# Weight tiles through GpSimd's queue, and a new order of work in the first two pairs of a fused attention and MLP kernel

## Chip, cores and metric

The kernel runs on one core of one Trainium2 chip. The metric is device time in microseconds (us) of one execution. The kernel before took 503.27 us, the median of three runs (502.56 to 503.57). The profile shown here is of one more execution.

## What is computed

Attention, then two feed-forward blocks on its output, all in float32 at the interface:

```
q, k, v: 2 x 12 heads x 448 x 64;  scale = 1/8
scores = scale * q @ k.T, causal mask (-1e9), softmax, @ v      # per head
x  = heads joined: 896 tokens x 768
h  = max(max(x @ w1, x @ w2), x @ w3);   y = h @ w_out          # 768 x 768 each
r  = max(y @ w_in, 0);  g = s * r * r + b                        # 768 x 2048
out = g @ w_out2                                                 # 2048 x 768
```

## The kernel before

**Tiles.** Two heads make a pair (12 pairs); a pair's q and k lie as one tile `R`, 128 partitions (2 heads x 64) by 2 x 448. Each float32 operand of a product is split into a rounded high part and a low remainder, and a product is the sum of three: high x high, low x high, high x low (`PARTS`). For a pair the tile `HL` holds -scale*q high, its low, k high and its low. `split_now` makes it for pair 0, in two column ranges (0 to 256, 256 to 448), `split_hi_early`/`split_lo_early` for pair 1, `scaled`, `split_hi` and `split_lo` for later pairs: GpSimd scales q in place (`R<-R`), VectorE casts the high parts (`CAST HL<-R`, L309), GpSimd subtracts the low parts (L92) and copies the tail columns into a block-diagonal tile `bd` (L296).

**Scores.** Query rows go in three tiles of 128 (tile 0, 1, 2) and a tail of 64 rows of both heads together. Tiles 0 and 1 lie in the PSUM bank pair `B`, tile 2 in `A`, the tail in `C`; each has one buffer, so the next pair's mask product (L350, L358, L365), which opens a bank, waits until ScalarE has read the old one. Per pair: masks and score products on TensorE, row minima of the negated scores on VectorE (`mx`, L396), exponentials with row sums on ScalarE (`p`, L408), 16 transposes on TensorE (L435) in four groups of four, copies of these (`PT`, three by ScalarE, one by VectorE, L441), products with V into the bank `o` (L451, L455, L460).

**The division.** Row sums are inverted, transposed into PSUM (L480), copied to `rows` (L487), sent by DMA to a DRAM row `rcd` (L488, L489), and from there by DMA to all partitions as `rb` (L497); VectorE multiplies `o` by `rb` into `xf` (L506), which frees `o` for the next product with V, and GpSimd splits `xf` into the `x` that the feed-forward part reads.

**Order.** Everything is written out by hand; each engine runs its instructions in that order. `step(s)` does, for s = 0 to 13, the scores of pair s (`new`), transposes of pair s-1 (`old`), products with V of pair s-2 (`out`), and the multiplication by `rb` of pair s-3; splitting of pair s+2 (`nxt`) and the scaling of pair s+3 lie beside them. All loads are issued by SyncE (SP) in program order: the pairs' `R` (L268), V in 42 pieces (L289, `V_LOADS` says how many at which place of a step), the weights' raw tiles `wraw` (`fetch_w`, L129, 768 KB each). SP has eight semaphores for its DMAs in turn, so an issue also waits for the DMA eight issues earlier. Within the attention part six raw tiles are fetched: at step 0 and at steps 1, 4, 8, 10, 11 (`FETCH`). In steps 1 to 13 four weight tiles are decoded between the attention work (`MID`, `END`).

**Feed-forward part.** From 93 us to the end TensorE runs the products of L698 and L807; the other 50 raw tiles are fetched by SP as decoding proceeds. `keep_busy` issues products on constants: `WARM` = 10 at the start, `BUSY` = 7 in step 0.

Of the kernel before, what the change touches and what calls it, by code (L numbers as in the profile page):

```python
# [14 lines left out]
ALU = mybir.AluOpType  # L15
# [8 lines left out]
TQ = 128  # L24
NQ = 3
# [14 lines left out]
V_LOADS = ((7, 7), (2, 5), (3, 4), (3, 0), (3, 0), (3, 0), (3, 0), (2, 0))  # L40
FILL = {12: (3, 5), 13: (0, 4)}
WARM = 10
BUSY = (7,)
# [7 lines left out]
def kernel(  # L51
# [73 lines left out]
    def fetch_w():  # L125
        if w_src:
            src = w_src.pop(0)
            raw = wr_p.tile([128, DM], I64, tag="wraw", name="wraw")
            nc.sync.dma_start(out=raw, in_=src)  # L129
            raws.append(raw)  # L130
# [101 lines left out]
    def attention():  # L232
        with ExitStack() as c2:
# [88 lines left out]
            def split_lo_early(p):  # L322
                HL, R = pair[p]["HL"], pair[p]["R"]
                nc.vector.scalar_tensor_tensor(
                    out=HL[:, 1], in0=R[:, 0], scalar=-scale, in1=HL[:, 0].bitcast(F32),
                    op0=ALU.mult, op1=ALU.subtract,
                )
                sub_lo(nc.vector, HL[:, 3], R[:, 1], HL[:, 2])

            def split_now(p, a, b, eng):  # L330
                HL, R = pair[p]["HL"], pair[p]["R"]
                q, k = (R[:, n, a:b] for n in range(2))
                qh, ql, kh, kl = (HL[:, n, a:b] for n in range(4))
                nc.vector.tensor_scalar(out=qh, in0=q, scalar1=-scale, scalar2=None, op0=ALU.mult)
                nc.scalar.copy(out=kh, in_=k)
                nc.vector.scalar_tensor_tensor(
                    out=ql, in0=q, scalar=-scale, in1=qh.bitcast(F32),
                    op0=ALU.mult, op1=ALU.subtract,
                )
                sub_lo(eng, kl, k, kh)  # L340
# [34 lines left out]
            def scores_ab(p, i):  # L375
                HL = pair[p]["HL"]
                n = (i + 1) * TQ
                for a, c in PARTS:
                    for h in range(2):
                        nc.tensor.matmul(  # L380
                            at(p, i)[:, h], HL[hs[h], a, i * TQ:n], HL[hs[h], 2 + c, 0:n],
                            start=False, stop=(a, c) == PARTS[-1], skip_group_check=True,
                        )
# [133 lines left out]
            for p in range(1, 4):  # L517
                load(p)
# [17 lines left out]
            split_now(0, 0, CUT, nc.vector)  # L536
            split_now(0, CUT, S, nc.gpsimd)
            both_tails(0)
            split_hi_early(1)
            first = early_products()  # L540
# [10 lines left out]
            def step(s):  # L551
# [4 lines left out]
                if new is not None:  # L556
                    results(new)
                    if new == 0:
                        mask_b(new)
                        scores_ab(new, 0)  # L560
                        scores_ab(new, 1)
                        mask_a(new)
                        scores_ab(new, 2)
                    else:
                        mask_a(new)
                        if new > 2:
                            mask_b(new)
                        scores_ab(new, 2)
                    if new == 2:
                        mask_b(new)  # L570
                    if new > 1:
                        scores_ab(new, 1)
                        scores_ab(new, 0)
                    if new != 1:
                        mask_c(new)
                        scores_c(new)
                else:
                    early(FILL[s][0])
                if old is not None:
                    transposes(old, 0)  # L580
                    transposes(old, 1)
                if new == 1:
                    mask_b(new)
                    scores_ab(new, 1)
                    scores_ab(new, 0)
                    mask_c(new)
                    scores_c(new)
                if new == 0:
                    for i in (0, 1, 2, NQ):
                        minima(new, i)  # L590
                    split_lo_early(1)
                    both_tails(1)
                    for n in (2, 3):
                        scaled(n)
                    for V in vs[:2]:
                        nc.gpsimd.memset(V[D:128, :, :, NQ, :], 0.0)
                elif new is not None:
                    minima(new, 2)
                if old is not None:
                    inverses(old)  # L600
                if new == 1:
# [3 lines left out]
                    for V in vs[2:]:  # L605
# [5 lines left out]
                if new == 1:  # L611
                    pt_copy(old, 0, nc.scalar)
                    pt_copy(old, 1, nc.scalar)
                    exps(new, 2)
# [22 lines left out]
                if new is not None:  # L637
                    for i in (1, 0) if new == 1 else (0, 1):
                        exps(new, i)
                if new == 0:  # L640
                    exps(new, 2)
# [6 lines left out]
                if new == 0:  # L648
                    load_v(loads[0])
# [5 lines left out]
                else:  # L655
                    fetch_w()
                load_v(loads[1])
                if s in FETCH:
                    fetch_w()
# [3 lines left out]
                if new == 1:  # L663
# [3 lines left out]
                    scaled(s + 3)  # L667
                if old is not None:
# [211 lines left out]
```

## Time and profile before

| what | value |
|---|---|
| median of the runs | 503.27 us |
| the profiled execution | 502.06 us |
| its span | 500.3 us |
| TensorE busy | 493.3 us (99%) |
| VectorE / ScalarE / GpSimd busy | 340.5 / 282.9 / 71.4 us |
| granted TensorE clock over the span | 0.999 |
| DMA moved, mean | 58.34 MB, 117 GB/s |

The span runs from the first to the last instruction; 1.76 us of the execution lie outside it. Engines work at the same time, so busy times don't add up. GpSimd's 71.4 us all lie in the first 97 us. In rows of a timeline the bracket at the end is idle time of that engine just before the row, and what ended it. A step of the attention part is told by TensorE's first mask product of it: step 1 starts at 10.03 us, step 2 at 14.89, steps 3 to 9 at 21.88, 28.26, 35.86, 43.10, 49.50, 55.87 and 62.29.

### The profile page before, as it was taken

What the parts mean: (1) busy time and instruction counts of PE and PEld (TensorE: products, weight loads), DVE (VectorE), ACT (ScalarE), POOL (GpSimd) and SP (SyncE); (2) the same over time, 40 slices, a digit from 0 to 9 for tenths busy, and PEclk for the clock granted to TensorE, in tenths of its full rate; (3) what the DMA queues carried; (4) which work ended last, traced back from release to release, by engine and by line L of the source; (5) the groups of instructions that cost most, each with busy time, mean ns of one, the idle gap of its engine ahead of it and who ended that gap; (6) DMA issues with size and microseconds to landing.
All of it is one profiled execution on the core that took longest, in us unless ns stands there. A gap on an engine that the chain in (4) does not pass through costs nothing.

```text
span 500.3 us, 7557 instructions
## 1 busy us (share of the span) xinstructions
PE 493.3 (99%) x2909; PEld 452.7 (90%) x2909; DVE 340.5 (68%) x512; ACT 282.9 (57%) x527; POOL 71.4 (14%) x103
## 2 busy tenths in 40 slices
PE   8999999999999999999999999999999999999997
PEld 4877888899999999999999999999999999999996
DVE  5778896665857667587677888888888644484401
ACT  5988977444445254444546878888786432253101
POOL 6988992300000000000000000000000000000000
PEclk9999999999999999999999999999999999999999
DMA  5777534223324231333223323332333323261003
GB/s 170 225 215 226 151 102 117 103 91 127 126 75 148 94 126 64 126 128 126 101 89 126 127 73 118 126 104 85 127 126 109 119 89 128 88 220 56 1 0 111
DMA packets 26212, 58.34 MB, mean 117 GB/s; under 512 B 13548, under 2 KB 17600, under 8 KB 26176
## 3 DMA queue, kind: packets, MB, share of 16 engines
q1 hardware_dynamic: 26032, 57.76, 35.2%
q8 instruction: 23, 0.38, 0.3%
q14 instruction: 13, 0.11, 0.1%
q10 hardware_dynamic: 144, 0.10, 0.1%
HBM read 55.05 MB, written 2.80 MB: 116 GB/s over the span
## 4 chain that ended last, share of the span: by engine, by line
PE 91%; DMA 2%; DVE 2%; SPq 2%; ACT 1%; POOL 1%; issue 0%; DVEq 0%; ACTq 0%
PE m L698 58%; PE m L807 23%; PE t L435 3%; PE o L451 2%; ACT p L408 1%; PE o L455 1%; SPq L289 1%; PE A L380 1%; PE C L388 1%; PE B L380 1%; DMA rcd<-rows 1%; DMA rb<-rcd 1%; DMA R<-in_qk_dram 1%; POOL HL L92 0%; PE o L460 0%
## 5 line engine op out<-in xcount | busy, mean ns | idle before, releaser
L698 PE MATMUL m<-x,whi 128*128 128x448 f32 x816 | 232.0, 366 | 0.0
L698 PEld LDWEIGHTS m<-x,whi 128*128 128x128 f32 x816 | 153.1, 188 | 12.3 <-ACT p L408 0.2
L698 PE MATMUL m<-x,wlo 128*128 128x448 f32 x408 | 149.0, 365 | 0.0
L807 PE MATMUL m<-whi,g 128*128 128x384 f32 x448 | 114.0, 334 | 0.0
L184 ACT CAST whi<-wa 128x768 fp32r<-128x768 f32 x56 | 46.7, 833 | 67.0 <-PE m L807 43.8
L698 PEld LDWEIGHTS m<-x,wlo 128*128 128x128 f32 x408 | 76.6, 188 | 6.0
L807 PEld LDWEIGHTS m<-whi,g 128*128 128x128 f32 x448 | 81.0, 188 | 0.0
L144 ACT ACTIVATE wa<-wraw 128x768 f32<-128x768 f32 x56 | 50.6, 904 | 52.3 <-DVE wlo L92 52.3
L92 DVE TENSOR_TENSOR wlo<-wa,whi 128x768 fp32r<-128x768 f32 x56 | 53.3, 953 | 38.4 <-ACT whi L184 38.4
L807 PE MATMUL m<-wlo,g 128*128 128x384 f32 x224 | 74.8, 334 | 0.0
L179 DVE CUSTOM_DVE_ANT_0 wa<-wa,wr 128x1536 uint16<-128x1536 uint16 x56 | 53.6, 957 | 1.9
L172 DVE SCALAR_TENSOR_TENSOR wa<-wraw,wa 128x768 int32<-128x768 int32 x56 | 53.7, 959 | 0.0
L147 ACT ACTIVATE wr<-wraw 128x768 int32<-128x768 uint32 x56 | 50.6, 904 | 0.0
L807 PEld LDWEIGHTS m<-wlo,g 128*128 128x128 f32 x224 | 42.0, 188 | 0.0
L705 DVE TENSOR_TENSOR t<-t,m 128x448 f32<-128x448 f32 x24 | 14.9, 621 | 38.7 <-PE m L698 38.7
L698 PE MATMUL m<-h,whi 128*128 128x448 f32 x144 | 40.9, 365 | 0.0
L166 DVE TENSOR_SCALAR wa<-wa 128x768 int32<-128x768 int32 x56 | 32.2, 575 | 1.8
L92 POOL TENSOR_TENSOR HL<-R,HL 128x448 fp32r<-128x448 f32 (+1 forms) x21 | 29.9, 1443 | 3.2 <-DVE HL L309 2.1
L792 ACT ACTIVATE r<-m 128x448 f32<-128x448 f32 x32 | 17.4, 544 | 22.2 <-PE m L698 22.2
L698 PEld LDWEIGHTS m<-h,whi 128*128 128x128 f32 x144 | 27.1, 188 | 2.1
L158 DVE TENSOR_SCALAR wa<-wa 128x768 f32<-128x768 f32 x52 | 28.7, 552 | 0.0
L781 DVE SCALAR_TENSOR_TENSOR r<-m,r 128x448 f32<-128x448 f32 x32 | 20.0, 625 | 12.3 <-ACT r L792 12.3
(85 smaller groups left out, 551.2 us busy)
## 6 DMA issues: line engine op xcount, KB each, us to landing
wraw<-in_w_dram SPq DMA_DIRECT2D x56, 768.0 KB
R<-in_qk_dram SPq DMA_DIRECT2D x11, 448.0 KB
rb<-rcd SPq DMA_DIRECT2D x24, 112.0 KB
out_dram<-o SPq DMA_DIRECT2D x13, 192.0 KB
v<-in_v_dram SPq DMA_DIRECT2D x4, 96.0 KB
v<-in_v_dram SPq DMA_DIRECT2D x2, 168.0 KB
v<-in_v_dram SPq DMA_DIRECT2D x6, 48.0 KB
v<-in_v_dram SPq DMA_DIRECT2D x2, 144.0 KB
```

The source lines that it names most:

```text
L92: eng.tensor_tensor(out=lo, in0=full, in1=hi.bitcast(F32), op=ALU.subtract)
L144: nc.scalar.activation(out=e["f"], in_=e["high"].bitcast(F32), func=ACTF.Abs)
L147: nc.scalar.activation(out=e["r"], in_=e["low"].bitcast(U32), func=ACTF.Copy, scale=2.0 ** -29)
L158: nc.vector.tensor_scalar(out=e["f"], in0=e["f"], scalar1=UNDER, scalar2=OVER, op0=ALU.max, op1=ALU.min)
L166: nc.vector.tensor_scalar(out=a, in0=a, scalar1=3, scalar2=0x3FFFFFF8, op0=ALU.logical_shift_left, op1=ALU.bitwise_and,)
L172: nc.vector.scalar_tensor_tensor(out=e["a"], in0=e["high"], scalar=-0x40000000, in1=e["a"], op0=ALU.bitwise_and, op1=ALU.bitwise_or,)
L179: nc.vector.tensor_tensor(out=e["a"], in0=e["a"], in1=e["r"], op=ALU.add)
L184: nc.scalar.copy(out=e["hi"], in_=e["f"])
L698: nc.tensor.matmul(p, wt[w][:, ws], cols(act[i], a, b), start=(i == 0 and n == 0), stop=(i == len(act) - 1 and n == 2),)
L781: nc.vector.scalar_tensor_tensor(out=r, in0=p, scalar=0.0, in1=r, op0=ALU.max, op1=ALU.mult)
L792: after(0, lambda: nc.scalar.activation(out=r, in_=p, func=ACTF.Relu))
L807: nc.tensor.matmul(acc[t][:, 0:EH], gt[f][:, a, ts], w[:, ws], start=(f == 0 and n == 0), stop=(f == KG - 1 and n == 2),)
```

## The change

Raw weight tiles that were fetched within the attention part (six of 56) are issued by GpSimd, in its own queue of DMAs, and no longer by SP. V's pieces are loaded in another distribution: three of pair 0's pieces between the loads of pairs 1 and 2, four between those of pairs 2 and 3, and ten at step 0 after pair 4's load; none behind `rb` in step 2. The second column range of pair 0 has its scaled q made by ScalarE and its low k by VectorE (before: VectorE, GpSimd). Pair 0's score products for tiles 0 and 1 run the two parts that need the high k for both tiles, and then the third part. Minima and exponentials of pair 0 go tile by tile in the order 0, 2, 1, and the tail's minimum stands between the two subtractions for pair 1. In step 1 the scores of `B` stand ahead of pair 0's first eight transposes, and the exponentials of `A` ahead of ScalarE's two copies. The zeroing of V's unused rows moves to steps 1 to 3. `BUSY` is 5.

```diff
-V_LOADS = ((7, 7), (2, 5), (3, 4), (3, 0), (3, 0), (3, 0), (3, 0), (2, 0))
+V_LOADS = ((0, 10), (3, 5), (3, 0), (3, 0), (3, 0), (3, 0), (3, 0), (2, 0))
-BUSY = (7,)
+BUSY = (5,)
-    def fetch_w():
+    def fetch_w(queue=nc.sync):
-            nc.sync.dma_start(out=raw, in_=src)
+            queue.dma_start(out=raw, in_=src)
...
                     op0=ALU.mult, op1=ALU.subtract,
                 )
+                minima(0, NQ)
                 sub_lo(nc.vector, HL[:, 3], R[:, 1], HL[:, 2])
...
-            def split_now(p, a, b, eng):
+            def split_now(p, a, b):
-                nc.vector.tensor_scalar(out=qh, in0=q, scalar1=-scale, scalar2=None, op0=ALU.mult)
                 nc.scalar.copy(out=kh, in_=k)
+                if a:
+                    nc.scalar.mul(out=qh, in_=q, mul=-scale)
+                    sub_lo(nc.vector, kl, k, kh)
+                else:
+                    nc.vector.tensor_scalar(
+                        out=qh, in0=q, scalar1=-scale, scalar2=None, op0=ALU.mult
+                    )
...
-                sub_lo(eng, kl, k, kh)
+                if not a:
+                    sub_lo(nc.vector, kl, k, kh)
...
-            def scores_ab(p, i):
+            def scores_ab(p, *tiles):
+                for parts in (PARTS[:2], PARTS[2:]):
+                    for i in tiles:
+                        n = (i + 1) * TQ
+                        for a, c in parts:
...
-            for p in range(1, 4):
-                load(p)
+            load(1)
+            load_v(3)
+            load(2)
+            load_v(4)
+            load(3)
...
-            split_now(0, 0, CUT, nc.vector)
-            split_now(0, CUT, S, nc.gpsimd)
+            split_now(0, 0, CUT)
+            split_now(0, CUT, S)
             both_tails(0)
             split_hi_early(1)
+            fetch_w(nc.gpsimd)
...
-                        scores_ab(new, 0)
-                        scores_ab(new, 1)
+                        scores_ab(new, 0, 1)
...
+                if new == 1:
+                    mask_b(new)
+                    scores_ab(new, 1)
+                    scores_ab(new, 0)
                 if old is not None:
                     transposes(old, 0)
                     transposes(old, 1)
                 if new == 1:
-                    mask_b(new)
-                    scores_ab(new, 1)
-                    scores_ab(new, 0)
                     mask_c(new)
                     scores_c(new)
                 if new == 0:
-                    for i in (0, 1, 2, NQ):
+                    for i in (0, 2, 1):
                         minima(new, i)
+                        exps(new, i)
...
                 if new == 1:
+                    exps(new, 2)
                     pt_copy(old, 0, nc.scalar)
                     pt_copy(old, 1, nc.scalar)
-                    exps(new, 2)
...
-                else:
-                    fetch_w()
                 load_v(loads[1])
-                if s in FETCH:
-                    fetch_w()
...
+                if s in FETCH:
+                    fetch_w(nc.gpsimd)
+                if 2 <= s < len(vs):
+                    nc.gpsimd.memset(vs[s][D:128, :, :, NQ, :], 0.0)
```

TensorE's queue at the start of step 1 (`A`, `B`, `C` are pair 1's banks, `t` pair 0's transposes), before:

```order
L350 LDWEIGHTS identb
L350 MATMUL A<-tri,identb 128x128
L380 MATMUL A<-HL 128x384 x6
L435 MATMUL t<-ident,p_133 128x128 x8
L358 LDWEIGHTS identb
L358 MATMUL B<-tri,identb 128x256
L358 LDWEIGHTS identb
L358 MATMUL B<-tri,identb 128x256
L380 MATMUL B<-HL 128x256 x6
L380 MATMUL B<-HL 128x128 x6
L365 LDWEIGHTS identb
L365 MATMUL C<-tri_106,identb 128x64
```

and now:

```order
L358 LDWEIGHTS identb
L358 MATMUL A<-tri,identb 128x128
L390 MATMUL A<-HL 128x384 x6
L366 LDWEIGHTS identb
L366 MATMUL B<-tri,identb 128x256
L366 LDWEIGHTS identb
L366 MATMUL B<-tri,identb 128x256
L390 MATMUL B<-HL 128x256 x6
L390 MATMUL B<-HL 128x128 x6
L445 MATMUL t<-ident,p_133 128x128 x8
L373 LDWEIGHTS identb
L373 MATMUL C<-tri_106,identb 128x64
```

The eight transposes, which need all exponentials of pair 0's tiles and the tail, stand behind `B`'s scores.

GpSimd's queue from pair 1's high parts to the scaling of pair 4 (`v_112` to `v_115` are the four groups of V), before:

```order
L296 TENSOR_SCALAR HL<-R 128x448 x2
L296 TENSOR_SCALAR bd_108<-HL 64x2x64 x2
L296 TENSOR_SCALAR R<-R 128x448 x2
L596 MEMSET v_112 64x2x64
L596 MEMSET v_113 64x2x64
L92 TENSOR_TENSOR HL<-R,HL 128x448 x2
L296 TENSOR_SCALAR bd_109<-HL 64x2x64 x2
L606 MEMSET v_114 64x8x64
L606 MEMSET v_115 64x12x64
L92 TENSOR_TENSOR HL<-R,HL 128x448 x2
L296 TENSOR_SCALAR bd_107<-HL 64x2x64 x2
L296 TENSOR_SCALAR R<-R 128x448
```

and now:

```order
L296 TENSOR_SCALAR HL<-R 128x448 x2
L129 DMA wraw<-in_w_dram 128x768
L296 TENSOR_SCALAR bd_108<-HL 64x2x64 x2
L296 TENSOR_SCALAR R<-R 128x448 x2
L92 TENSOR_TENSOR HL<-R,HL 128x448 x2
L296 TENSOR_SCALAR bd_109<-HL 64x2x64 x2
L619 MEMSET v_112 64x2x64
L619 MEMSET v_113 64x2x64
L92 TENSOR_TENSOR HL<-R,HL 128x448 x2
L296 TENSOR_SCALAR bd_107<-HL 64x2x64 x2
L296 TENSOR_SCALAR R<-R 128x448
L129 DMA wraw<-in_w_dram 128x768
```

Two DMA issues have come in, and the zeroing of groups 114 and 115 has gone to later steps. Four more issues follow, at the ends of steps 4, 8, 10 and 11.

SP's queue around the first two divisions, before:

```order
L289 DMA v_114<-in_v_dram 32x4x64
L129 DMA wraw<-in_w_dram 128x768
L488 DMA rcd<-rows 7x128
L489 DMA rcd<-rows 1x64
L268 DMA R<-in_qk_dram 128x896
L289 DMA v_114<-in_v_dram 32x4x64
L289 DMA v_114<-in_v_dram 80x4x64 x2
L497 DMA rb<-rcd 64x448 x2
L289 DMA v_114<-in_v_dram 48x4x64 x2
L289 DMA v_114<-in_v_dram 64x4x64 x2
L488 DMA rcd<-rows 7x128
```

and now:

```order
L289 DMA v_114<-in_v_dram 80x4x64 x2
L289 DMA v_114<-in_v_dram 48x4x64
L498 DMA rcd<-rows 7x128
L499 DMA rcd<-rows 1x64
L268 DMA R<-in_qk_dram 128x896
L289 DMA v_114<-in_v_dram 48x4x64
L289 DMA v_114<-in_v_dram 64x4x64 x2
L507 DMA rb<-rcd 64x448 x2
L498 DMA rcd<-rows 7x128
```

The first `rcd` in each is pair 1's, the last pair 2's. The raw tile ahead of pair 1's `rcd` and the four pieces of V between pair 1's `rb` and pair 2's `rcd` are gone from there.

## Rows read from the trace of the kernel before

**Rows 1.** Waits of TensorE, 0 to 130 us: total us, times, longest.

```profile
PE o L451 <- DVE xf L506: 1.9, 2, 1.1
...
PE A L350 <- ACT p L408: 0.6, 1, 0.6
```

**Rows 2.** Stretches: length; busy PE, PEld, DVE, ACT, POOL; clock; DMA share, GB/s.

```profile
6.00:8.00 2.00, 2.00 (x14) 1.22 (x13) 1.99 (x5) 0.86 (x5) 0.58 (x2) 1.00 0.92 321
...
15.00:22.00 7.00, 6.87 (x69) 5.37 (x67) 4.79 (x11) 6.97 (x26) 5.86 (x11) 1.00 0.70 199
...
28.30:35.90 7.60, 6.52 (x68) 5.36 (x66) 5.60 (x11) 6.22 (x20) 5.73 (x8) 1.00 0.58 147
35.90:43.10 7.20, 6.42 (x67) 5.29 (x65) 5.67 (x11) 6.17 (x20) 5.83 (x8) 1.00 0.91 222
...
49.50:55.90 6.40, 6.40 (x68) 5.34 (x66) 5.41 (x11) 6.15 (x20) 6.16 (x8) 1.00 0.65 172
```

**Rows 3.** Timeline of DVE around the divisions and casts: start, length, instruction, idle before.

```profile
27.58 0.28 DVE L487 COPY rows<-A 7x128 f32<-7x128 f32 x1 [0.47 <-PE A L480]
...
32.21 0.62 DVE L506 TENSOR_TENSOR xf<-o,rb 128x448 f32<-128x448 f32 x1 [1.64 <-DMA rb<-rcd]
...
39.53 0.62 DVE L506 TENSOR_TENSOR xf<-o,rb 128x448 f32<-128x448 f32 x1 [1.33 <-DMA rb<-rcd]
...
47.29 0.70 DVE L309 CAST HL<-R 128x896 fp32r<-128x896 f32 x1
48.82 0.28 DVE L487 COPY rows<-A 7x128 f32<-7x128 f32 x1 [0.83 <-PE A L480]
```

**Rows 4.** Chain that ended last, in time: start, us, what.

```profile
16.23 1.15 POOL v L606 x2
...
23.07 3.99 DMA rcd<-rows
...
32.13 0.45 SPq L488
```

**Rows 5.** Timeline of SP's queue: a V piece, a raw tile, one quiet division.

```profile
8.20 0.57 SPq L289 DMA_DIRECT2D v<-in_v_dram  x1
...
22.57 0.41 SPq L129 DMA_DIRECT2D wraw<-in_w_dram  x1
...
68.31 0.27 SPq L488 DMA_DIRECT2D rcd<-rows  x1
...
69.50 1.10 SPq L497 DMA_DIRECT2D rb<-rcd  x2
```

**Rows 6.** Timeline of GpSimd: pair 1's high parts, pair 2's low parts, pair 8's scaling.

```profile
8.32 1.09 POOL L296 TENSOR_SCALAR HL<-R 128x448 fp32r<-128x448 f32 x2 [1.38 <-DMA R<-in_qk_dram]
...
12.99 2.24 POOL L92 TENSOR_TENSOR HL<-R,HL 128x448 fp32r<-128x448 f32 x2
...
46.42 0.56 POOL L296 TENSOR_SCALAR R<-R 128x448 f32<-128x448 f32 x1
```

**Rows 7.** Timeline of ScalarE: pair 0's exponentials of tile 1, tile 2.

```profile
7.84 0.47 ACT L408 ACTIVATE p<-B,mx 128x256 f32<-128x256 f32 x1
...
8.74 0.59 ACT L408 ACTIVATE p<-A,mx 128x384 f32<-128x384 f32 x1
```

**Rows 8.** Timeline of TensorE in steps 0 to 2.

```profile
7.72 1.70 PE L513 MATMUL warm<-const-bfloat16-1.0 128*128 128x512 bf16 x7
10.03 0.27 PE L350 MATMUL A<-tri,identb 128*128 128x128 bf16 x2 [0.61 <-ACT p L408]
...
14.89 0.28 PE L350 MATMUL A<-tri,identb 128*128 128x128 bf16 x2
...
16.02 0.38 PE L358 MATMUL B<-tri,identb 128*128 128x256 bf16 x2
```

**Rows 9.** SP's issues of raw tiles: ns, least, median, most.

```profile
L129 SPq DMA_DIRECT2D wraw<-in_w_dram x7: 362/534/582, 11.4 to 97.5; - x7
```

**Rows 10.** GpSimd's low parts, 14.9 to 75 us: ns, least, median, most.

```profile
L92 POOL TENSOR_TENSOR HL<-R,HL x19: 1137/1457/2042, 14.1 to 70.4; 128x448 fp32r<-128x448 f32 x19
```

More of the change, by code (lines that the diff above doesn't have):

```diff
@@ L373, in at @@
                 return pair[p]["A" if i == 2 else "B"][:, :, a:b]
-            def scores_ab(p, i):
+            def scores_ab(p, *tiles):
                 HL = pair[p]["HL"]
[L377 to L383, printed above, removed]
+                for parts in (PARTS[:2], PARTS[2:]):
+                    for i in tiles:
+                        n = (i + 1) * TQ
+                        for a, c in parts:
+                            for h in range(2):
+                                nc.tensor.matmul(
+                                    at(p, i)[:, h], HL[hs[h], a, i * TQ:n], HL[hs[h], 2 + c, 0:n],
+                                    start=False, stop=(a, c) == PARTS[-1], skip_group_check=True,
+                                )
             def scores_c(p):
@@ L594, in step @@
                         scaled(n)
-                    for V in vs[:2]:
-                        nc.gpsimd.memset(V[D:128, :, :, NQ, :], 0.0)
                 elif new is not None:
@@ L604, in step @@
                     both_tails(2)
-                    for V in vs[2:]:
+                    for V in vs[:2]:
                         nc.gpsimd.memset(V[D:128, :, :, NQ, :], 0.0)
@@ L636, in step @@
                     pv_out(out)
-                if new is not None:
+                if new:
                     for i in (1, 0) if new == 1 else (0, 1):
                         exps(new, i)
-                if new == 0:
-                    exps(new, 2)
                 if old is not None:
@@ L647, in step @@
                     transposes(old, 3)
-                if new == 0:
-                    load_v(loads[0])
                 if s + 4 < n_pairs:
```

## The prediction, made before the changed kernel had run

> **What bounds the kernel now.** I read the waits of TensorE first. It is busy in 493.3 of 500.3 us, and over the first 130 us, where everything lies that the change touches, it waits for few things: 1.9 us in two waits of the product with V for `xf`, and 0.6 us once at the start of step 1 for ScalarE, which still holds `A` [rows 1]. From 93 us on its products follow each other without a gap, and the change doesn't reach them. So TensorE's order is the path, and a gain can only be time that a step of the attention part takes above its undisturbed length. The stretches give this length: step 7 takes 6.40 us, all busy. Step 4 takes 7.60 and step 5 takes 7.20, with 1.08 and 0.78 us not busy; step 2 takes about 7.0 [rows 2]. Steps 4 and 5 are thus 1.20 and 0.80 us too long. Why is told by VectorE's timeline: it stands 1.64 us before `xf` at 32.21 and 1.33 us before the one at 39.53, for the DMA of `rb` [rows 3], and `o` is not free before. The chain of waits leads on: pair 1's `rcd` takes 3.99 us to land from 23.07, and pair 2's `rcd` is issued at 32.13 [rows 4], although VectorE had its `rows` at 27.86 (27.58 + 0.28) [rows 3]: SP was still at four pieces of V. The last views are the timelines of GpSimd and ScalarE in steps 0 and 1. GpSimd is hardly freer than TensorE, 6.16 of 6.40 us busy in step 7, ScalarE 6.15 [rows 2]; both matter below.
>
> **The divisions (steps 4 and 5).** Pair 1's `rcd` carries 3.5 KB and needs 3.99 us behind five pieces of V and the 768 KB tile that SP issued at 22.57 [rows 5]. The same DMA at 68.31, with little else moving, has landed when `rb` is issued at 69.50, 1.2 us later [rows 5]. Now no raw tile stands in this queue; the V pieces ahead of it stay. I take 2.3 us, between the two ends but nearer the quiet one, since the tile is most of the bytes in front. That is 1.7 us less, and the issue on SP is not held by the tile's 0.41 us. `rb` then lands some 2.1 us earlier against TensorE's order, more than the 1.64 us that VectorE stood; but if the steps before get shorter by 1.1 us (below), `xf` is wanted earlier too, and 0.6 us of the standing would remain, of which TensorE sees less (1.64 became 1.08). I count 1.0 of the 1.20 us as gained, bounds 0.2 and 1.2. In step 5 pair 2's `rcd` is no longer behind four pieces of V: it can go at 27.9 instead of 32.13, 4.3 us earlier, where 1.33 are wanted. All 0.80 us go, lower bound 0.4. What is late next in both steps is nothing on TensorE; VectorE has 0.83 us of standing per step [rows 3].
>
> The Trainium skill speaks against this part: by its page "DMA: Bandwidth & Descriptors", section "Issuing engines are not separate DMA queues", DMAs of all issuing engines share the same 16 DMA engines and interleave, and a second issuer only saves the time of issuing. By it `rcd` keeps its 3.99 us and only the 0.41 us of the issue go. The row shows that the two DMAs' times overlap, not in which order packets go, so it can't refute that; it is the second rival.
>
> **The head (steps 0 and 1).** Before, ScalarE did pair 0's tiles in the order 0, 1, 2, tail, and `A` (tile 2) was held by it nearly to the end; TensorE opened pair 1's `A` at 10.03, after 0.61 us of standing [rows 8]. With tile 2 ahead of tile 1, `A` is free 0.90 us earlier (the two exponentials of tile 1 run from 7.84 to 8.74 [rows 7]). The two products of `keep_busy` that go are 2 x 0.243 = 0.49 us [rows 8], so TensorE gets there at about 8.9 without and 8.5 with them gone. But `A` also needs pair 1's low parts. VectorE now does pair 0's minima first, the tail's too, then k's low part. The high parts come from GpSimd at 8.32, after 1.38 us of standing for pair 1's load [rows 6]; SP's piece of V at 8.20 waited for the same DMA [rows 5]. Before, pairs 1, 2 and 3 (448 KB each) were in the queue together, and pair 1 landed when most of all three had moved. Now 112 KB of V stand between pair 1 and pair 2. At 321 GB/s [rows 2] the 784 KB that no longer share its time are 2.4 us; I take 2.0, so it lands at about 6.2; bounds 0 and 2.4. Then GpSimd, with pair 0's tail copies first, has the high parts at about 7.7; VectorE reaches the low part of q at 7.8, after the minima, and k's at 9.5. `A`'s last third goes at 9.6, `B`'s scores (0.9 us) follow where before the transposes stood, and the transposes, which need the tail's exponential (9.9), no longer wait. Every later instruction of step 1 is the same, and step 2 begins at about 13.5 instead of 14.89 [rows 8]: 1.4 us. Pair 0's second range on VectorE and ScalarE instead of GpSimd gives the same order of readiness, and is in this figure.
>
> Against it stands GpSimd: pair 2's low parts, which step 2 needs, follow the scaling of pairs 2 and 3, and pair 3's load is now issued four pieces of V later, beside the first raw tile. Before, they ran from 12.99 to 15.23 [rows 6]. I expect pair 3 at 11.5 and the low parts done at 14.4, so 0.3 us of the 1.4 are lost at step 2. If pair 3 comes at 12.5, nearly all is. Head: 1.1 us gained, bounds 0.2 and 1.5. Step 2's own 0.6 us above a normal step stay: its `B` opens at 16.02 when ScalarE has finished pair 1's [rows 8], and that moves with the rest. Bounds 0 and 0.5.
>
> **GpSimd's issues.** No GpSimd DMA is in this trace. The nearest row below is the same tile's issue on SP, 0.53 us median, 0.36 least [rows 9]; above it GpSimd's longest instruction, 2.04 us [rows 10]. I take 1.0, in the nearer half, as GpSimd must do it between its own instructions. Behind it wait, in order, `bd`, the scaling and the low parts. Three issues come before pair 8's scaling, which ended at 46.98 [rows 6]; what GpSimd stands in steps 4 and 5 (1.87 + 1.37 = 3.2 us [rows 2], much of it for `xf` and casts that now come earlier) and an earlier start by some 1.5 us pay for them, so that it ends at about 45.0. VectorE's cast of pair 8 was at 47.29 [rows 3] and is wanted 2.9 us earlier (1.1 + 1.0 + 0.8), at 44.4. It waits 0.6 us, hidden by the 0.83 us that VectorE stands before `rows` [rows 3]. In steps 8 to 10, where VectorE also decodes, I count 0.3 us lost. The later zeroing of V (1.15 us [rows 4]) is in GpSimd's sum. The issues at steps 8, 10 and 11 come where its results are wanted over 2 us later: nothing.
>
> **Sum.** -1.1 (head) - 1.0 (step 4) - 0.8 (step 5) + 0.3 (GpSimd) = -2.6 us. On the profiled execution, 502.06 us with 1.76 outside its span, that is 499.5. It lies 1.2 us below the median of the runs, 503.27, and nothing says that the changed runs lie low, so the predicted time is 503.27 - 2.6 = 500.7 us.
>
> **Rivals.**
> 1. Pair 3 comes late and the head gains nothing. For it: three big loads and the raw tile now compete between 8 and 12 us, when the DMA engines were 92% busy before at 6 to 8 us [rows 2]. Against it: the total of bytes before step 2 hardly differs. -0.2 - 1.0 - 0.8 + 0.3 = -1.7: 501.6 us.
> 2. The raw tiles delay `rcd` and `rb` from the other queue as much as from this one. Step 4 keeps 0.8 of its 1.20 us, step 5 still gains, since its wait was on SP's order: -1.1 - 0.4 - 0.8 + 0.3 = -2.0, 501.3 us. With a late pair 3 too, -1.1: 502.2 us.
> 3. GpSimd becomes the bound (slower). Three issues at more than about 1.15 us each use up what is left of VectorE's standing (0.83 - 0.6) and the 0.25 us that ScalarE has free per step [rows 2]; from there each further 0.1 us per issue costs TensorE 0.3 us. At 2.1 us per issue the whole gain is gone, at 2.5 the kernel is 1.2 us slower: 504.5 us. For it: GpSimd is 96% busy in step 7, and its low parts take 1.14 us alone and up to 2.04 beside VectorE [rows 10]. Against it: even its longest instruction is under 2.1. The Trainium skill has a rule for this: by "SBUF — State Buffer", section "SBUF: two separate sides", a DMA from GpSimd's queue can't have its descriptors written while VectorE runs a two-port copy; it gives 3.1 us where 0.62 is usual, and advises SP or ScalarE. By its figure the three issues would take 9.3 us, and the kernel would be slower by some 3.0 us. The trace agrees that the two engines hinder each other, by the spread of 1.14 to 2.04 us, but has no such DMA.
> 4. No change: the standing moves, the waits for `rb` go but `xf` or ScalarE's exponentials hold the same bank a little later. Speaks for it that ScalarE is 96% busy; against it that it stands before its exponentials in steps 4 and 5 for the same `xf`. 503.0 us.
>
> **Chances.** Forecast 0.50; rival 1 0.17; rival 2 0.13 (a third of it together with the first); rival 3 0.08, of which 0.05 end slower than by 0.2%; rival 4 0.12. A measurement of this kernel can tell about 0.2%, 1.0 us. Faster by more: 0.50 + 0.17 + 0.12, and 0.01 of rival 3, 0.80. Same: 0.14. Slower: 0.06. The range: all upper bounds together, -1.5 - 0.5 - 1.2 - 0.8, are -4.0, which gives 499.3; the upper end, 503.1, takes in rivals 1, 2 and most of 4, and leaves out rival 3. The forecast's own range is 499.8 to 501.5.
>
> **What would show it.** The step lengths of TensorE: steps 4 and 5 at 6.4 to 6.6 us with no wait of `o` for `xf`; step 2 beginning at 13.4 to 14.1. Pair 1's load ends GpSimd's standing at 6 to 7 us. `rcd` of pair 1 lands in 2 to 2.5 us; pair 2's is issued right behind its `rows`. The issue on GpSimd costs about 1 us of its time, and VectorE's cast waits for the scaling from step 6 on. I'm wrong if `xf` still waits for `rb`, if step 2 begins after 14.6, or if VectorE waits for GpSimd by more than its standing in steps 6 to 10, seen as steps longer than 6.40.

## The result: slower, and the profile after

The changed kernel takes 505.51 us (median of 5 runs, 504.35 to 508.14) where the kernel before, in runs beside it, takes 502.74 (502.12 to 503.57). The ratio is 1.0065, with an interval of 1.0048 to 1.0081. The forecast was faster, 500.7 us.

The page's busy times after; before, TensorE was busy 493.3 us and the span was 500.3:

```profile
span 503.8 us, 7566 instructions
...
PE 495.0 (98%) x2907; PEld 453.8 (90%) x2907; DVE 341.1 (68%) x512; ACT 283.0 (56%) x528; POOL 74.8 (15%) x108
```

TensorE issues two products on constants fewer (`BUSY` is 5, not 7) and otherwise the same ones, yet it is busy 1.7 us longer: somewhere it ran at a lower clock. The granted clock over the span is 0.996 to 0.998 in all five runs, where the profile before has 0.999. Its waits after, 0 to 130 us (total us, times, longest), beside [rows 1]:

```profile
PE o L461 <- DVE xf L516: 3.5, 2, 3.3
```

One wait of 3.3 us has taken the place of two of about 1 us. The stretches after, one for each of steps 2 and 3, three parts of step 3, and step 4 (columns as in [rows 2]: length; busy PE, PEld, DVE, ACT, POOL; granted clock; DMA share, GB/s):

```profile
14.95:21.83 6.88, 6.75 (x67) 5.36 (x65) 5.33 (x11) 6.85 (x26) 6.51 (x12) 1.00 0.52 135
21.83:33.29 11.46, 8.16 (x68) 6.38 (x65) 6.56 (x11) 6.48 (x22) 7.66 (x10) 0.85 0.76 196
25.00:28.70 3.70, 0.45 (x5) 0.21 (x2) 0.64 (x2) 1.79 (x6) 0.92 (x2) 1.00 0.84 166
28.70:31.00 2.30, 2.26 (x10) 1.34 (x12) 2.30 (x4) 1.35 (x7) 1.70 (x2) 0.53 0.73 232
31.00:33.30 2.30, 2.30 (x24) 2.07 (x22) 0.79 (x3) 0.61 (x3) 2.05 (x2) 0.73 0.56 150
33.30:39.70 6.40, 6.40 (x68) 5.34 (x66) 5.89 (x11) 6.16 (x20) 5.08 (x8) 1.00 0.63 168
```

Step 2 begins at 14.95 (14.89 before, [rows 8]): the head gave nothing. Step 3 takes 11.46 us; before it was, in the same columns:

```profile
21.88:28.26 6.38, 6.38 (x67) 5.31 (x66) 5.91 (x11) 6.27 (x21) 6.14 (x8) 1.00 0.86 256
```

The DMA engines were 86% busy there, which left little room for anything added. Steps 4 and 5 take 6.38 and 6.39 (7.60 and 7.24 before). So by step 6: +5.1 in step 3, -2.1 in steps 4 and 5, -0.1 in step 2, and 0.1 in the head: 3.0 us later. The other 0.5 us of the span is lost after that. Within step 3, TensorE is nearly idle to 28.7, and then its granted clock is 0.53, about the lower of its two levels (1.2 of 2.4 GHz). Two rows of its timeline, the product with V in step 3 and in step 4:

```profile
28.74 0.96 PE L461 MATMUL o<-PT,v 128*64 128x448 f32 x1 [3.29 <-DVE xf L516]
...
36.77 0.59 PE L461 MATMUL o<-PT,v 128*64 128x448 f32 x1
```

The same product takes 0.96 us in place of 0.59. What `xf` waited for is in VectorE's timeline after, to be read beside [rows 3]:

```profile
28.06 0.62 DVE L516 TENSOR_TENSOR xf<-o,rb 128x448 f32<-128x448 f32 x1 [3.39 <-DMA rb<-rcd]
...
35.52 0.57 DVE L516 TENSOR_TENSOR xf<-o,rb 128x448 f32<-128x448 f32 x1
...
51.78 0.28 DVE L497 COPY rows<-A 7x128 f32<-7x128 f32 x1 [0.84 <-PE A L490]
```

It is pair 0's `rb`. The chain of waits after (start, us, what), beside [rows 4], leads back from there:

```profile
9.00 7.80 DMA v<-in_v_dram
...
17.77 0.33 SPq L498
...
20.38 0.50 SPq L507
20.98 6.99 DMA rb<-rcd
28.06 0.64 DVE xf L516
```

And GpSimd's timeline has the issue of the second raw tile just ahead of it, and the other two of the first 50 us:

```profile
8.79 0.75 POOL L129 DMA_DIRECT2D wraw<-in_w_dram  x1
...
20.26 0.84 POOL L129 DMA_DIRECT2D wraw<-in_w_dram  x1
...
42.86 0.60 POOL L129 DMA_DIRECT2D wraw<-in_w_dram  x1
```

`rb` (two pieces of 112 KB) is issued 0.1 us behind a tile of 768 KB in the other queue, and its second piece takes 6.99 us to land. The tile itself takes 7.3, so the two are under way together (DMA issues, 18 to 30 us):

```profile
wraw<-in_w_dram POOLq DMA_DIRECT2D x1, 768.0 KB, 7.3
```

Before, the same `rb` and the product that needs it were (SP's timeline, then VectorE's):

```profile
16.43 0.48 SPq L488 DMA_DIRECT2D rcd<-rows  x1
...
18.74 1.14 SPq L497 DMA_DIRECT2D rb<-rcd  x2
```

```profile
24.19 0.56 DVE L506 TENSOR_TENSOR xf<-o,rb 128x448 f32<-128x448 f32 x1
```

`xf` didn't stand at all, so the second piece of `rb`, whose issue began at 19.34, had landed 4.85 us behind that (24.19 - 19.34) or sooner. After, `rb` is issued 1.6 us later, mostly since SP is at its ten pieces of V in step 0 until 17.67 (one of them takes the 7.80 us of the chain, issued 0.2 us behind the first tile), and it needs at least 2.1 us more.

### The profile page after: what moved, and what is told of

It is laid out like the page before. It is cut to its first block, busy times and chain, and to the rows that moved or that the text cites. A ratio compares the mean times of both kernels' runs of the same rounds, so it can differ in the third digit from the quotient of the medians.

```text
span 503.8 us, 7566 instructions
## 1 busy us (share of the span) xinstructions
PE 495.0 (98%) x2907; PEld 453.8 (90%) x2907; DVE 341.1 (68%) x512; ACT 283.0 (56%) x528; POOL 74.8 (15%) x108
## 4 chain that ended last, share of the span: by engine, by line
PE 92%; DMA 3%; SPq 2%; DVE 1%; ACT 1%; issue 1%; DVEq 0%
PE m L707 58%; PE m L816 23%; PE t L445 3%; PE o L461 2%; DMA v<-in_v_dram 2%; PE o L465 1%; DMA rb<-rcd 1%; SPq L289 1%; PE A L390 1%; PE C L398 1%; PE B L390 1%; SPq L268 1%; ACT p L418 1%; PE o L470 1%; PE B L366 0%
## 5 line engine op out<-in xcount | busy, mean ns | idle before, releaser
L714 DVE TENSOR_TENSOR t<-t,m 128x448 f32<-128x448 f32 x24 | 14.9, 621 | 38.7 <-PE m L707 38.7
L158 DVE TENSOR_SCALAR wa<-wa 128x768 f32<-128x768 f32 x52 | 28.7, 552 | 0.5 <-ACT wa L144 0.5
L461 PE MATMUL o<-PT,v 128*64 128x448 f32 (+3 forms) x96 | 25.0, 406 | 3.5 <-DVE xf L516 3.5
```

The costliest lines, as they stand in the source:

```text
L158: nc.vector.tensor_scalar(out=e["f"], in0=e["f"], scalar1=UNDER, scalar2=OVER, op0=ALU.max, op1=ALU.min)
L461: nc.tensor.matmul(o[hs[0], j * TQ:S], V[:, 0, j], PT[:, at:at + m * TQ + D], **flags)
```

## The experiments

All were timed in 5 rounds beside the kernel before; each ratio is to those runs (medians 502.31 to 503.26), not to the first row. "Stands" is VectorE's idle time ahead of `xf` in the profiled execution, in us, for steps 3, 4 and 5. It is one execution of each kernel, and the times of one kernel lie up to 7.4 us apart (e6):

| kernel | us | ratio to before (interval) | stands |
|---|---|---|---|
| before | 502.74 | 1 | 0, 1.64, 1.33 |
| after | 505.51 | 1.0065 (1.0048-1.0081) | 3.39, 0, 0 |
| e1 | 504.19 | 1.0035 (1.001-1.006) | 0, 2.08, 0 |
| e2 | 503.54 | 1.0016 (0.9997-1.0034) | 0.28, 2.98, 0 |
| e3 | 506.97 | 1.0073 (1.0052-1.0094) | 0, 0, 0.55 (1.82 in step 6) |
| e4 | 505.65 | 1.0047 (1.003-1.0063) | 4.34, 0.28, 0 |
| e5 | 506.35 | 1.0070 (1.0056-1.0084) | 0, 0.28, 0 |
| e6 | 505.66 | 1.0075 (1.0043-1.0106) | 1.30, 2.18, 0 |
| e7 | 503.12 | 1.0016 (1.0001-1.0031) | 0, 0.94, 2.02 |
| e8 | 502.47 | 0.9993 (0.9983-1.0003) | 0.58, 1.18, 2.31 |
| e9 | 503.45 | 1.0015 (1.0005-1.0024) | 2.43, 0.89, 0 |
| e10 | 502.45 | 0.9990 (0.9977-1.0003) | 0, 0, 0 |
| e11 | 507.06 | 1.0092 (1.0075-1.0109) | 0.52, 1.74, 0 |
| e12 | 500.24 | 0.9959 (0.9945-0.9973) | 0, 0, 0 |
| e13 | 501.12 | 0.9970 (0.9960-0.9981) | 0.63, 1.36, 0 |
| e14 | 500.62 | 0.9961 (0.9945-0.9976) | 0, 0.49, 0 |
| e15 | 501.58 | 0.9977 (0.9960-0.9995) | 0, 1.92, 0 |

The theory: a raw tile in a second queue takes its time from what is under way in the first, and the second tile meets pair 0's `rb`. The rivals: the issue costs GpSimd its time; the new order or the V loads are the cause; the low clock is the larger part.

### e1 and e2: the second, or every, raw tile back in SP's queue

```diff
 e1:
-                    fetch_w(nc.gpsimd)
+                    fetch_w(nc.sync if s == 1 else nc.gpsimd)
 e2, at both places:
-            fetch_w(nc.gpsimd)
+            fetch_w()
```

> The changed kernel with one raw tile, that of step 1, issued by SP again (at the end of step 1, as before); the other five stay in GpSimd's queue. Theory R (the raw tile of step 1, issued at 20.26 us in a queue of its own, takes the DMA engines' time from pair 0's rb, issued at 20.4 and landed only at 28.0): rb lands by 26, the standing of o for xf in step 3 falls from 3.3 to at most 1.2 us, the clock doesn't fall, and the time is 500 to 502 us. Theory V (the new places of V's pieces, ten of them at step 0, hold SP and fill its queue): rb still lands at 27 to 28, the standing stays near 3 us, 504.5 to 505.5 us.

> The changed kernel with all six raw tiles issued by SP at the changed places in the program; V's pieces and the order of work are the changed ones. Theory R: no standing over 1 us in step 3, 500 to 501.5 us. Theory V: step 3 stands by about 3 us as before in the changed kernel, 504.5 us or more.

Step 3 lost its standing in both profiles, and by the ratios the time fell by half and by three quarters of the loss. Both kernels have two groups of times: e1 seven runs of 502.5 to 504.4 us and five of 506.3 to 507.9, e2 seven of 501.9 to 503.6 and five of 505.1 to 506.2. e1's profile is of the lower group and e2's of the upper, so what the other group waited for isn't shown. Neither is faster than before: the standing is now in step 4, 2.08 and 2.98 us where before has 1.64. VectorE's timeline of e2:

```profile
25.12 0.62 DVE L516 TENSOR_TENSOR xf<-o,rb 128x448 f32<-128x448 f32 x1 [0.28 <-DMA rb<-rcd]
...
34.07 0.62 DVE L516 TENSOR_TENSOR xf<-o,rb 128x448 f32<-128x448 f32 x1 [2.98 <-DMA rb<-rcd]
```

In both, the second tile is ahead of pair 1's `rcd` in SP's queue again, as it was before, so step 4 isn't a test of the 1.0 us that the prediction counted there. In e1 step 2 also took 8.18 us, with GpSimd standing 2.34 us for pair 3's load: the prediction's first rival, seen here.

### e3: the kernel before with the second queue alone

```diff
-                if s in FETCH:
-                    fetch_w()
...
+                if s in FETCH:
+                    fetch_w(nc.gpsimd)
```

> The kernel before, with nothing changed but the six raw tiles issued in GpSimd's queue. Theory R: pair 0's rb, which is issued 1.6 us earlier here than in the changed kernel, is met by the raw tile of step 1 too: VectorE stands 0.5 to 2 us for it in step 3, where it didn't stand before, step 4 gets shorter by about 1 us, and the sum is 502.5 to 504 us. Theory V: no standing in step 3, and steps 4 and 5 gain 1 to 2 us: 501 to 502 us.

The queue alone costs all that the whole change costs. The standing is in another place, since the second issue falls at 23.13 here. The later tile, GpSimd's timeline and then VectorE's:

```profile
40.52 0.60 POOL L129 DMA_DIRECT2D wraw<-in_w_dram  x1
```

```profile
48.12 0.62 DVE L506 TENSOR_TENSOR xf<-o,rb 128x448 f32<-128x448 f32 x1 [1.82 <-DMA rb<-rcd]
```

That tile is issued 0.05 us ahead of pair 3's `rb`, whose second piece takes 6.89 us to land. In this profile the head is 2.3 us later too (step 1 begins at 12.36): the second part of pair 0's load came late, ahead of any raw tile. That lateness comes and goes between executions (below), so e3's profile overstates the queue's own part, and its time is the measure. By step 7 the profile is 2.2 us behind before, no more than the head: what its steps 5 and 6 stand is about what steps 4 and 5 of before stood. The queue's own part comes after: 0.8 us in steps 7 to 10, and 1.68 us in which TensorE waits at 89.69 for an `xf` whose `rb` (6.20 us from 82.73) meets the tile of step 11, issued at 83.56.

### e4: TensorE kept busy in step 3

```diff
-BUSY = (5,)
+BUSY = (5, 0, 0, 14)
```

> The changed kernel with 14 products on constants added in step 3, just ahead of the product with V that waits for xf, where TensorE stood 3.3 us. If the product with V ran at half speed (granted clock 0.53 from 28.7 to 31.0 us) because TensorE had stood, then the clock stays at 1.00, step 3 takes 9.3 to 9.8 us instead of 11.46, and the time falls by 1.5 to 1.9 us to 503.6 to 504. If the slow products have another cause, step 3 keeps its 11.4 us and the time its 505.5 us.

Columns as above, the two stretches of e4 around and behind the start of `xf` (29.48, after 4.34 us of standing):

```profile
28.70:31.00 2.30, 2.19 (x15) 0.91 (x14) 1.52 (x4) 0.00 (x0) 0.65 (x2) 1.00 0.28 46
31.00:33.30 2.30, 2.30 (x33) 2.07 (x29) 2.24 (x6) 2.20 (x9) 1.67 (x2) 1.00 0.82 249
```

The clock stays at 1.00, and the product with V takes 1.91 us in place of 3.56. Those 1.65 us are what the low clock costs in after's profile. The time hardly followed: 505.65 us, by the ratios 0.9 us less than after, with intervals that overlap, where 1.5 to 1.9 were expected. In the profiled execution `rb` came a microsecond later still, against the start of step 3 (7.83 us to land, the tile issued 0.2 us ahead of it). So the clock's part is shown by the rows, not by the times.

### e5: the raw tiles in ScalarE's queue

```diff
-                    fetch_w(nc.gpsimd)
+                    fetch_w(nc.scalar)
```

> The changed kernel with its six raw tiles issued in ScalarE's queue of DMAs in place of GpSimd's, at the same places of the program. Theory S (any second queue does it: the raw tile's packets take turns with those of rb in SP's queue): rb of pair 0 again lands 6 to 8 us after its issue, TensorE stands 2 to 4 us in step 3, 504.5 to 506.5 us. Theory G (it is peculiar to GpSimd's software queue): rb lands within 5 us, no standing over 1 us in step 3, 502.5 to 503.5 us.

As slow as after, without an issue on GpSimd, but not by the same wait. ScalarE reaches its issues at other times: the first tile goes out at 4.89 (8.79 in after), 0.2 us behind pair 2's load, and the second at 19.69, 5.8 us ahead of pair 0's `rb`, for which nothing stands. Here it is pair 2's load that comes late, and step 2 that pays: 11.5 us, with the granted clock at 0.55 from 21 to 26 us. GpSimd's timeline, the scaling of pairs 2 and 3:

```profile
13.97 0.56 POOL L296 TENSOR_SCALAR R<-R 128x448 f32<-128x448 f32 x1 [3.40 <-DMA R<-in_qk_dram]
15.16 0.56 POOL L296 TENSOR_SCALAR R<-R 128x448 f32<-128x448 f32 x1 [0.62 <-DMA R<-in_qk_dram]
```

A loss of this size thus needs neither GpSimd's issues nor a hindrance between it and VectorE. That ScalarE's queue would delay `rb` as GpSimd's does, e5 doesn't show, since its tile wasn't beside `rb`.

### e6, e7 and e8: the second tile half a step later, in either queue

```diff
 e6:
-FETCH = (1, 4, 8, 10, 11)
+FETCH = (2, 4, 8, 10, 11)
 END: high1 in step 4, low1 in 8
 e7: as e6, and all tiles on SP
 e8: as e7, and pair 3's scaling behind pair 2's low parts
-                    for n in (2, 3):
-                        scaled(n)
+                    scaled(2)
...
                     split_lo(2)
+                    scaled(3)
```

> The changed kernel with the second raw tile still in GpSimd's queue, but issued at the end of step 2 instead of step 1, when pair 0's rb has landed (its decoding moves with it: first half at the end of step 4, second at the end of step 8). Theory R (a raw tile in another queue delays the rb that is under way with it): step 3 loses its standing of 3.3 us and its 1.65 us at the lower clock; pair 1's rb, under way then, may stand up to 2 us in step 4: 501.5 to 503.5 us. Theory V: the standing of step 3 stays, 505 to 506 us.

> The changed kernel with all raw tiles issued by SP: the first where the kernel before had it (behind pair 4's load), the second behind pair 1's rb in step 2, with its decoding moved as in the run with the later tile. No raw tile then stands ahead of a rcd or rb of pairs 0 and 1, in either queue. If raw tiles near the divisions are the whole of the standing, steps 3 to 5 take 6.4 to 6.9 us each and the time is 500.5 to 502 us. If the V pieces still make rb late, step 3 or 4 keeps 1 us or more: 502.5 to 503.5 us.

> The run before it, and the scaling of pair 3's q moved behind pair 2's low parts in GpSimd's order. Where GpSimd waited for pair 3's load (2.1 to 2.3 us in the two runs with raw tiles on SP) TensorE stood 1.0 us in step 2 for pair 2's low parts. If that load was the cause, the standing in step 2 goes and the time is 0.7 to 1.2 us below the run before it. If GpSimd is late for another reason (its own sum of work), no difference over 0.3 us.

Most of the standing moves with the tile: from step 3 to step 4 in GpSimd's queue (e6, where step 3 keeps 1.30), to steps 4 and 5 in SP's (e7). It doesn't go, and e6 is as slow as after. e8 is no different from before. It was meant to mend a standing in step 2, but that step takes 6.87 us in the profiles of e7 and e8 alike; the 0.65 us between their medians are not explained.

### e9, e10 and e11: the second and third tile past step 4

```diff
-FETCH = (1, 4, 8, 10, 11)
+FETCH = (4, 6, 8, 10, 11)
 END: high1, low1 in steps 6, 7; high2 in 8; low2 in 9
```

> The kernel of e8 (after's order of work, all raw tiles in SP's queue), with the second raw tile asked for in step 4 and the third in step 6 in place of steps 2 and 4, and the decode of both moved behind them (high1 in step 6, high2 in step 8). Theory A (xf stands for rb where a raw tile stands beside rcd and rb between 15 and 45 us, whatever queue it is in): xf stands under 0.5 us in each of steps 3, 4 and 5, where e8 stood 0.58, 1.18 and 2.31; TensorE gains 2 to 3 us by step 6, some given back later by the decode; 499.5 to 501.5 us. Theory B (the rows are late for another reason: the loads of the pairs and of V in that stretch): the standing of steps 4 and 5 stays within 0.8 us of e8's, 502 to 503.5 us.

> The kernel before with the same change of steps for the second and third raw tile, and nothing else. Theory A: the standing of steps 4 and 5 of before (1.64 and 1.33 us ahead of xf, 1.0 and 0.8 of TensorE's steps) goes, 500.5 to 502 us, about 1 us over e9 if the order of the first two pairs is worth anything, the same as e9 if not. Theory B: 502.3 to 503.5 us, the standing stays.

> The changed kernel, raw tiles in GpSimd's queue as it has them, with the same change of steps for the second and third raw tile. Theory A (a tile in another queue costs what the transfers beside it wait, and nothing where none of these is waited for): the standing of 3.4 us in step 3 and the low clock behind it go, since no raw tile is under way from 14 to 35 us; 501 to 503 us, at most 1 us over e9, from the first tile beside the head's loads. Theory B (GpSimd's queue costs by itself, by its issues or by the later start of rcd behind V): step 3 still stands over 2 us, 504.5 to 506 us.

All three missed the time that the theory gave. e10 shows the mechanism and what was overlooked: steps 3 to 7 take 6.4 us each, 1.9 us gained by the start of step 8, and then step 8 takes 7.17 us and TensorE waits 1.3 us more in step 9. In step 8 it stands 0.29 us for V's last pieces, beside which the third tile now is (issued at 50.99; e12, without it, stands 0.16). The wait in step 9 is for `xf`, and `xf` is late by the decode of a tile, which VectorE has ahead of it and for which it stands. VectorE's timeline of e10:

```profile
63.24 1.19 DVE L153 SCALAR_TENSOR_TENSOR wa<-wa,over 128x768 f32<-128x768 f32 x1 [1.24 <-ACT wa L144]
```

So in e10 the decode, which moved with the tile, gives back more than V does. In e11 the third tile meets V's last pieces from GpSimd's queue. GpSimd's timeline, TensorE's, and the stretches of e11:

```profile
52.59 0.83 POOL L129 DMA_DIRECT2D wraw<-in_w_dram  x1
```

```profile
62.44 0.43 PE L461 MATMUL o<-PT,v 128*64 128x64 f32 x2 [2.33 <-DMA v<-in_v_dram]
```

```profile
60.10:62.40 2.30, 0.01 (x1) 0.00 (x0) 0.65 (x1) 0.72 (x4) 2.22 (x3) 1.00 0.48 98
62.40:65.00 2.60, 2.56 (x14) 2.38 (x15) 0.80 (x2) 0.63 (x2) 2.44 (x5) 0.53 0.02 6
```

Much of the bill of step 3 again, 2.3 us of standing and the clock at 0.53 behind it, but in step 8 and for V in place of `rb`. Up to step 3 e11 differs from after by the place of the second tile alone, and there `xf` stands 0.52 us in place of 3.39. This comparison holds over all profiles. From the start of the issue of the second piece of pair 0's `rb` to `xf` it is 7.1 us in after and 7.9 in e4, the two with a tile issued 0.1 to 0.2 us ahead of `rb` in another queue; in the six others that stood in step 3 (e2, e6, e8, e9, e11, e13) it is 2.9 to 4.6. My belief that only 15 to 45 us were crowded fell. In e9, `xf` of step 3 stood 2.43 us although the second tile was far away: its `rcd` went out at 18.21, behind ten pieces of V, at which SP had stood 2.5 us for the first tile. Part of this is the execution: e13 below is the same program up to there and stood 0.63, with `rcd` at 17.68 and step 3 begun 0.9 us later.

### e12, e13 and e14: no raw tile between steps 4 and 8, on SP

```diff
-FETCH = (1, 4, 8, 10, 11)
+FETCH = (4, 8, 9, 10, 12)
 END: high1, low1 in steps 6, 7; high2 in 9; low2, clamp2 in 10; shift2, sign2 in 11
 e13: the same in e8
 e14: as e13, and
-V_LOADS = ((0, 10), (3, 5), (3, 0), ...
+V_LOADS = ((0, 7), (3, 8), (3, 0), ...
```

> The kernel before, raw tiles in SP's queue, the second asked for in step 4 (as in e10) and the others in steps 8, 9, 10 and 12, so that none is under way beside V's pieces of steps 5 to 7; the decode of the third moved to steps 9 to 12. Theory A (what stands for a DMA stands where a raw tile is under way beside it, and nowhere else): steps 2 to 7 take 6.4 us each as in e10, and the 1.3 to 1.6 us that e10 lost in steps 7 and 8 are not lost: 500.3 to 501.3 us. Theory C (the end of the attention is bound by something else, the decode or the other loads, so that what steps 4 and 5 gain is given back whatever is moved): 502.0 to 503.3 us, with the loss of e10 again by step 9.

> The same steps for the raw tiles in the kernel of e8, which has after's order of the first two pairs and its V loads (ten pieces of V behind the first raw tile in step 0). Theory A: as e9 up to step 7 (xf stands 2.4 in step 3 and 0.9 in step 4, because rcd of pair 0 goes out at 18.2 behind the ten pieces), without e9's loss of 1 us in step 8: 501.5 to 502.7 us, over e12. Theory C: 503 to 504 us.

> e13 with seven pieces of V in step 0 in place of ten, and eight in place of five behind rb in step 1. If the ten pieces in one go are what holds pair 0's rcd back (it went out at 15.8 to 16.4 us in the kernels with seven there, at 17.8 to 18.2 with ten), rcd goes out by 16.5, rb lands 1.5 us earlier, xf of step 3 stands under 1 us, and the time is 0.8 to 1.5 us under e13's, 500 to 501.3 us: then after's order is worth half a us or more over e12. If not, rcd goes out as late as in e13 and the times agree within 0.4 us.

e12 came out as the theory said, 2.1 us faster than before, and beats both kernels. It moves the third tile's decode too, away from where it held `xf` in e10, so what it gains over e10 isn't all due to the tiles. In e12 TensorE waits for no `xf` from 0 to 130 us, and its steps 4 and 5 are:

```profile
29.16:35.54 6.38, 6.38 (x68) 5.32 (x65) 5.12 (x11) 5.34 (x19) 6.14 (x8) 1.00 0.67 167
35.54:41.93 6.39, 6.39 (x68) 5.32 (x65) 5.38 (x11) 5.34 (x19) 6.14 (x8) 1.00 0.79 206
```

That another bound gives every gain back, the rival here, is refuted. e14 against e13: with seven pieces in step 0 `rcd` of pair 0 goes out at 15.75 in place of 17.68 and step 3 doesn't stand; the time is 0.5 us lower, less than forecast. e14 (500.62) isn't faster than e12 (500.24): the changed order is worth nothing measurable over the old one even with all that mended.

### e15: e14 with GpSimd's queue

```diff
-                    fetch_w()
+                    fetch_w(nc.gpsimd)
```

> e14 with its six raw tiles in GpSimd's queue, the first at the place where the changed kernel has it, the others in steps 4, 8, 9, 10 and 12. Theory A (GpSimd's queue costs only what the transfers beside the tile make something wait): no standing over 0.5 us in steps 3 and 4, since no raw tile is under way from 15 to 35 us, steps of 6.4 to 6.5 us up to step 8 but step 5 or 6 (beside the tile of step 4: up to 1.5), 500.5 to 502.5 us. Theory D (the queue itself costs: its issues on GpSimd, or work in SP's queue slowed for the whole stretch): 503.5 us or more, as the changed kernel less its standing in step 3.

The first tile goes out where after has it. 501.58 us, faster than before: the second queue by itself doesn't cost the 3 us. It stood 1.92 us in step 4, where I expected under 0.5 and where no raw tile was under way (issues at 8.13 and 39.13). Of the kernels with the changed order and the tiles past step 4, all stand there, 0.49 to 1.92; of those with the old one, none does. No run was made to find what holds `rb` there, but the rows show one part: pair 1's `rcd` goes out 2.6 to 4.0 us after its `rows` are there (e9, e11, e13, e14, e15), as SP is still at V's pieces; in e10 and e12 it is 0.6 to 0.7. Nor is the 1.0 us over e14 explained; their intervals overlap.

## Why the prediction was wrong

- **The step that failed** is in the part on the divisions: "Now no raw tile stands in this queue". From there it reckoned `rcd` and `rb` as freed of the tile. The tile had only changed its queue; its 768 KB were still under way, for 7.3 us, and SP's `rb`, issued 0.1 us behind it, took 6.99. The second rival named this mechanism, but priced it at 0.6 us and in step 4 alone; it cost 5.1 us in step 3, of which 3.3 are standing and 1.65 the low clock. In the sum, step 3 stood at nothing. The prediction looked only at the waits that were there before. For pair 0's `rb`, which had none, it asked neither when it was issued nor what would now stand beside it.
- **A second miss in the same place:** the ten pieces of V in step 0 hold SP until 17.7 us and pair 0's `rcd` by 1.3 us. The sum had every issue that V gave up behind `rb`, and none where they went to.
- **Steps 4 and 5** have the forecast length (6.4), but not for the forecast reason: after a step 3 that is 5 us late, `rb` had time. With no raw tile near (e9, e11, e13 to e15) step 4 still stands 0.49 to 1.92 us, where the prediction left 0.6. For step 5 there is no standing in e1 and e2, as forecast. But e10 and e12 have none either, and they keep the four pieces of V ahead of pair 2's `rcd` that the prediction blamed: its reason for step 5 isn't shown.
- **The head** was sized at 1.1 us and gave none. Pair 1's load did come earlier, GpSimd taking it at 7.74 without standing (8.32 before). Where GpSimd stood for it (e1, e2, e11, e13, e15) it came at 7.0 to 7.4: about 1 us earlier than before, where 2.0 were reckoned. And ScalarE stood for the second part of pair 0's load, which it had not done before:

```profile
5.81 0.35 ACT L335 CAST HL<-R 128x192 fp32r<-128x192 f32 x1 [1.40 <-DMA R<-in_qk_dram]
```

  In the profiles of e1, e2, e11 and e15 that part was in time, and step 2 began at 14.10 to 14.43, 0.5 to 0.8 us earlier than before. In those of after, e3 and e14 it was late. But it isn't the whole: in e6, e7 and e13 it was in time too, and step 2 began at 14.90 to 15.13. There the ten products on constants that open TensorE's queue took 4.42 to 4.43 us, in e1, e2, e11 and e15 3.61 to 4.15. Before, and after:

```profile
0.77 3.98 PE L513 MATMUL warm<-const-bfloat16-1.0 128*128 128x512 bf16 x10 [0.77 <-PEq L866]
```

```profile
0.77 4.36 PE L523 MATMUL warm<-const-bfloat16-1.0 128*128 128x512 bf16 x10 [0.77 <-PEq L875]
```

  So 0.4 us of the head's missing gain came from the execution. What makes the load or these products late is open. And e1 and e2 then lost the gain in step 2 to pair 3's load, the first rival, and e5 to pair 2's.
- **GpSimd's issues** were sized at 1.0 us, for a loss of 0.3. They take 0.60 to 0.84 us, and VectorE still stands 0.84 us ahead of `rows` at the end of step 6, as before (0.83, [rows 3]): nothing was lost there. The third rival fell. The Trainium skill's "SBUF — State Buffer", section "SBUF: two separate sides", gives 3.1 us for a whole DMA from GpSimd's queue beside a copy of VectorE; the prediction had used it as the time of the issue on GpSimd, and as that none of the six issues shows it. The rule of the Trainium skill's "DMA: Bandwidth & Descriptors", section "Issuing engines are not separate DMA queues", is that all issuers share the 16 DMA engines. The rows of after, e3 and e5 agree with it: `rb` and pair 2's load were late beside a tile of another queue. I weighed it as a rival to a gain of 0.6 us, when it spoke against the change's first premise.
- **The range** left out rival 3 and any loss in a step that had been undisturbed. With 0.06 for slower, the chances trusted that a transfer moved to another queue is out of the way.

## What to carry to other kernels

A large transfer that moves to another queue leaves the first queue's order, not its transfers: list every small transfer that will be under way beside it, with its slack, including those that nobody waits for today. Place large loads where nothing small and urgent stands beside them, as in e12: new places for raw tiles and their decode, a few numbers in two tables, gained 0.4%, where the new queue and the new order together lost 0.65%. A standing of TensorE can cost once more behind it: read the granted clock of the stretch after a wait before you size it.

## What the runs showed of the hardware that was not expected

- GpSimd's issue of a 768 KB DMA keeps it 0.60 us (median of six, to 0.84); ScalarE's of the same tile took 0.33 to 0.38 (e5). The tile took 5.7 us to land, in the median of after:

```profile
wraw<-in_w_dram POOLq DMA_DIRECT2D x6, 768.0 KB, 5.7
```

- TensorE's granted clock was 0.53 right behind 3.3 us of standing (after, step 3) and behind 2.3 us (e11, step 8). Behind the standings of about 1 us in steps 4 and 5 before it stayed at 1.00 [rows 2].
- The same ten products that open TensorE's queue took 3.61 us in one execution (e15) and 4.43 in others (e6, e7, e14).
